# A convolution and a feed-forward block in one kernel: signal parts kept in the signal's place, a joint weight factor, joined butterflies, and the roots of four more row tiles on ScalarE

## The chip, the core and the metric

The kernel runs on one core of one Trainium2 chip. The metric is the device time of one execution in microseconds. Of three runs of the kernel before, the median was 1249.17 us, the lowest 1248.23 and the highest 1249.23. Below, PE is TensorE, DVE is VectorE, ACT is ScalarE, POOL is GpSimd (which here issues the DMAs that add to memory) and SP is the queue that issues all other DMAs.

## The reference

With x = A_q (2048 rows, 1024 columns, float32) and xn its layer norm along the columns, the result is the sum of three terms:

```
y   = causal conv over 2048 rows, per channel, of (short conv of k) * v with ssm_k
out = x + xn * (y + (short conv of k) * v * ssm_D)
        + silu(xn @ w1) @ w2            # w1 1024 x 3584, w2 3584 x 1024
```

The short convolution has four taps per channel. The long one is defined by FFTs of length 4096 along the rows.

## The kernel before, in words

All matmuls take float16 operands; to keep float32 accuracy each operand is stored as two float16 parts, hi and lo (the helper split, L370: ScalarE writes hi, VectorE writes lo = source times scale minus hi), and each product is three matmuls: hi hi, hi lo, lo hi. All instructions are recorded by a small planner written in the kernel (class Order). Each piece of work is a Python generator, a stream, that yields operations with a cost guess; the planner emits, again and again, the stream head that can start earliest, less a bias per stream. Flags and ring buffers with tokens hold a stream back. The order on each engine is thus a result of the planner's costs and of which buffers are free, and it is fixed when the program is built. Since helpers record the instructions, most rows of the profile bear the helper's line: L349 is a tensor_tensor, L352 a scalar_tensor_tensor, L360 an activation, L336 a DMA on SP, L342 a DMA with transpose on SP, L346 a DMA on GpSimd.

**Opening.** ln_rows takes the 16 row tiles of x in groups of 2, 2, 4 and 8. For each tile it forms mean and variance (tiles 4 and 5 on ScalarE, the others on VectorE), then the reciprocal root of the group: for tiles 0 to 3 a Sqrt on ScalarE and a reciprocal on VectorE (L564), for the others an eleven-instruction chain on VectorE (L549 to L559). Tiles 4 to 7 are normalized by ScalarE, the others by VectorE. turned transposes tiles on TensorE into three PSUM buffers ft (L598) and splits them into the operands x2, x3, x4 and so on. Meanwhile the first 8 products of the feed-forward run (plain_unit, L958 to L960), whose results are taken out of the PSUM banks ff by silu. Sqrt and Silu lie in different function tables of ScalarE, so a table load stands between them.

**First matrix product.** units runs it as Strassen-Winograd products P1 to P7 of blocks of x and w1, 12 matmuls of 512 columns each. factors_w1 forms the weight factors (B11; T2 and T3; B21 and B22; T1; T4) for each of 14 pairs of column blocks, stores them in the six buffers wo and keeps a copy in memory for the second half. evacuate copies and combines the products.

**Convolution.** It runs beside the two matrix products, for eight groups g of 128 channels. Per group: loads brings k (kin) and the kernel ssm_k (kf); load_v brings v; gate applies the taps and multiplies by v into acc, and sums squares for the scales; signal_parts splits acc and kf into hi and lo, by DMA transposes via cm; stage1 multiplies them by the transform's matrix on TensorE (L1581 to L1583) and to_spec copies the PSUM tiles into spec and tmp; forward, product and inverse are butterflies and a complex product on VectorE; stage1_inv (L1772 to L1774) transforms back, gated multiplies by the normalized x, and the result is stored or added to out. acc has one buffer; hi and lo have two each, which also serve as the places for quarters of v.

**Second matrix product.** The plain part (L1101 to L1103) and then eight units of P1 to P7 (units2). evacuate2 takes each unit's products out of PSUM: a from P6, d from P5, and direct copies of P2 and P3; they go to half buffers hf (three pairs), and GpSimd adds them to out in memory. In the last unit, direct copies may also use the two pairs ht; d may not (L1214, ws_r is hf).

## Time and profile before

| | |
|---|---|
| median of three runs | 1249.17 us |
| profiled execution, its own time | 1247.09 us |
| its span | 1245.0 us |
| TensorE busy | 1232.0 us, 99% |
| VectorE busy | 1118.5 us, 90% |
| ScalarE busy | 788.4 us, 63% |
| granted TensorE clock, mean | 1.0 |

A row of a timeline gives the start and length in us, the engine, the line, the operation, out and in, how many were merged, and in brackets how long the engine sat idle before it and which instruction or DMA ended that. A row of waits gives who waited for whom, the total, how often, and the longest. A row of groups gives the count, the busy time in us and the mean of one in ns.

### The profile page before, as it was taken

What the parts mean: (1) busy time and instruction counts of PE and PEld (TensorE: products, weight loads), DVE (VectorE), ACT (ScalarE), POOL (GpSimd) and SP (SyncE); (2) the same over time, 40 slices, a digit from 0 to 9 for tenths busy, and PEclk for the clock granted to TensorE, in tenths of its full rate; (3) what the DMA queues carried; (4) which work ended last, traced back from release to release, by engine and by line L of the source; (5) the groups of instructions that cost most, each with busy time, mean ns of one, the idle gap of its engine ahead of it and who ended that gap; (6) DMA issues with size and microseconds to landing.
All of it is one profiled execution on the core that took longest, in us unless ns stands there. A gap on an engine that the chain in (4) does not pass through costs nothing. (4 is left out here: it accounts for less than half of the span.)

```text
span 1245.0 us, 17285 instructions
## 1 busy us (share of the span) xinstructions
PE 1232.0 (99%) x6092; PEld 601.9 (48%) x6092; DVE 1118.5 (90%) x1360; ACT 788.4 (63%) x1431; POOL 83.6 (7%) x93
## 2 busy tenths in 40 slices
PE   9999999999999999999999999999999999999997
PEld 8544444444444544444444544544544444454453
DVE  7999996996999789999999799899999889997981
ACT  7778888876688878669563823753453464554252
POOL 0000000000000000000000000000120030123223
PEclk9999999999999999999999999999999999999999
DMA  9376998879799899859984665579496498978757
GB/s 368 102 263 233 321 302 296 287 233 200 227 327 286 247 294 338 225 168 281 354 304 131 172 214 135 168 263 258 106 225 178 117 195 237 256 142 154 157 121 103
DMA packets 272807, 279.84 MB, mean 225 GB/s; under 512 B 73808, under 2 KB 192848, under 8 KB 271440
## 3 DMA queue, kind: packets, MB, share of 16 engines
q1 hardware_dynamic: 256992, 262.22, 68.2%
q0 software_dynamic: 15728, 16.52, 10.0%
q8 instruction: 47, 0.77, 0.2%
q14 instruction: 40, 0.33, 0.1%
HBM read 175.66 MB, written 88.34 MB: 212 GB/s over the span
## 5 line engine op out<-in xcount | busy, mean ns | idle before, releaser
L1101 PE MATMUL ff<-x,wo 128*128 128x512 f16 x868 | 328.1, 378 | 2.8 <-ACT hf L360 2.2
L1103 PE MATMUL ff<-x,wo 128*128 128x512 f16 x868 | 328.1, 378 | 0.0
L1102 PE MATMUL ff<-x,wo 128*128 128x512 f16 x868 | 328.1, 378 | 0.0
L958 PE MATMUL ff<-x,wo 128*128 128x512 f16 (+1 forms) x808 | 302.8, 375 | 1.3 <-DVE hf L349 0.9
L960 PE MATMUL ff<-x,wo 128*128 128x512 f16 (+1 forms) x808 | 302.8, 375 | 0.0
L959 PE MATMUL ff<-x,wo 128*128 128x512 f16 (+1 forms) x808 | 302.8, 375 | 0.0
L349 DVE TENSOR_TENSOR spec<-spec 128x512 f32<-128x512 f32 (+2 forms) x256 | 261.5, 1052 | 2.1
L1102 PEld LDWEIGHTS <-wo 128*128 128x128 f16 x868 | 84.9, 98 | 101.9 <-issue 3.3
L1103 PEld LDWEIGHTS <-wo 128*128 128x128 f16 x868 | 84.9, 98 | 101.6
L1101 PEld LDWEIGHTS <-wo 128*128 128x128 f16 x868 | 85.8, 99 | 98.8
L960 PEld LDWEIGHTS <-wo 128*128 128x128 f16 x808 | 79.0, 98 | 92.1
L958 PEld LDWEIGHTS <-wo 128*128 128x128 f16 x808 | 80.4, 100 | 87.9
L959 PEld LDWEIGHTS <-wo 128*128 128x128 f16 x808 | 79.0, 98 | 89.8 <-issue 1.9
L349 DVE TENSOR_TENSOR tmp<-spec 128x2048 f32<-128x2048 f32 (+1 forms) x48 | 92.7, 1933 | 0.9
L352 DVE SCALAR_TENSOR_TENSOR ht<-hf,wsc,ht 128x1024 f16<-128x1024 f32 (+1 forms) x56 | 67.3, 1203 | 7.0 <-ACT ht L360 5.3
L360 ACT ACTIVATE ht<-hf,wsc 128x1024 f16<-128x1024 f32 (+1 forms) x56 | 60.8, 1085 | 8.5 <-DMA hs<-ht 3.5
L352 DVE SCALAR_TENSOR_TENSOR wo<-raw,wsc,wo 128x512 f16<-128x512 f32 (+1 forms) x56 | 56.5, 1013 | 7.3 <-ACT wo L360 6.9
L360 ACT ACTIVATE spec<-spec 128x1024 bf16<-128x1024 f32 x32 | 33.7, 1054 | 45.6 <-DVE spec L349 45.6
L352 DVE SCALAR_TENSOR_TENSOR acc<-kin,taps,acc 128x1024 f32<-128x1024 f32 x48 | 61.4, 1279 | 0.6 <-ACT acc L360 0.5
L349 DVE TENSOR_TENSOR spec<-tmp 128x512 f32<-128x512 f32 (+1 forms) x80 | 60.9, 793 | 0.9
L346 POOL DMA_DIRECT2D kf<-in_dskip x8 | 7.4, 922 | 801.8 <-DMA kf<-in_fs 327.2
L346 POOL DMA_DIRECT2D out<-hf x45 | 40.7, 911 | 298.5 <-ACT hf L360 201.8
(193 smaller groups left out, 1798.7 us busy)
## 6 DMA issues: line engine op xcount, KB each, us to landing
wo<-hs SPq DMA_DIRECT2D x160, 256.0 KB, 3.5
hs<-ht SPq DMA_DIRECT2D x80, 256.0 KB, 4.3
raw<-in_w SPq DMA_DIRECT2D x28, 512.0 KB, 5.8
wraw<-in_w SPq DMA_DIRECT2D x24, 512.0 KB, 5.8
w2n<-in_w SPq DMA_DIRECT2D x24, 512.0 KB, 5.9
out<-hf POOLq DMA_DIRECT2D x45, 256.0 KB, 4.3
kin<-in_kp SPq DMA_DIRECT2D x16, 704.0 KB, 5.1
xt<-in_x SPq DMA_DIRECT2D x16, 512.0 KB, 7.4
```

The source lines that it names most:

```text
L346: return Op("POOL", 1.1, 3.0, lambda: nc.gpsimd.dma_start(o, i, accum_op=ADD), [i], [o], m, 2.3 * n)
L349: return V(lambda: nc.vector.tensor_tensor(o, a, b, op=op), o, [a, b], **k)
L352: return V(lambda: nc.vector.scalar_tensor_tensor(o, a, s, b, op0=op0, op1=op1), o, [a, b] + ([] if isinstance(s, float) else [s]), **k)
L360: nc.scalar.activation(o, i, func, scale=scale, **kw)
L958: nc.tensor.matmul(o, w[:, 0, k], xf[:, :, k, 0], start=first and k == 0, stop=False, **kw)
L959: nc.tensor.matmul(o, w[:, 0, k], xf[:, :, k, 1], start=False, stop=False, **kw)
L960: nc.tensor.matmul(o, w[:, 1, k], xf[:, :, k, 0], start=False, stop=last and k == KH - 1, **kw)
L1101: nc.tensor.matmul(po, hx[:, n, 0, :], wc[:, n, 0, :], start=first and n == 0, stop=False, **kw)
L1102: nc.tensor.matmul(po, hx[:, n, 0, :], wc[:, n, 1, :], start=False, stop=False, **kw)
L1103: nc.tensor.matmul(po, hx[:, n, 1, :], wc[:, n, 0, :], start=False, stop=last and n == 3, **kw)
```

## The change

Four things are changed. (1) The roots of row tiles 4 to 7 go to ScalarE and a reciprocal as for tiles 0 to 3, and every Silu waits, in the planner, for that root. (2) T1 is no longer formed in a buffer of its own: B21 and B22 are turned into T4 and T1 by one subtraction of the same T2 from both, and split as one operand of double width; one subtraction per pair goes. (3) One tile sig holds acc and v; the f16 parts of the transposed signal are written over acc, and those of kf over v, by one split of 2048 elements in place of four of 512. v comes in halves, not quarters, and is multiplied and squared in halves. gate and load_v of a group wait for the last matmul of the first stage of the group before. (4) Butterflies on VectorE are joined: the order of the planes in spec (table AT) is changed so that fewer and longer instructions cover the same elements. Besides, in the last unit d may use a half of ht (the function place).

```diff
-ROOTED = 4
+ROOTED = 8
...
-FACTORS = (("B11",), ("T2", "T3"), ("B21", "B22"), ("T1",), ("T4",))
+FACTORS = (("B11",), ("T2", "T3"), ("B21", "B22"), ("T4", "T1"))
...
-    t1_r = Ring(order, rawa, "t1", 1)
...
                 yield V(lambda: nc.vector.reciprocal(r, v), r, [v], us=0.18)
+                if t0 + n == ROOTED:
+                    flag["rooted"].set()
...
             yield from part(("B11",), b[0, 0])
-            yield t1_r.ready
-            t1, t1k = t1_r.tile([P, KH, P])
-            yield v_tt(t1, b[0, 1], b[0, 0], SUB)
             yield v_tt(b[0, 1], b[1, 1], b[0, 1], SUB)
             yield v_tt(b[0, 0], b[0, 1], b[0, 0], ADD)
             yield from part(("T2", "T3"), hv[0])
             yield from part(("B21", "B22"), hv[1])
-            yield from part(("T1",), t1)
-            t1k.set()
-            yield v_tt(b[1, 0], b[1, 0], b[0, 0], SUB)
+            two = hv[1].rearrange("p k (f w) -> p k f w", f=2)
+            yield v_tt(two, two, again(b[0, 0]), SUB)
             toks[0].set()
-            yield from part(("T4",), b[1, 0])
+            yield from part(("T4", "T1"), hv[1])
             toks[1].set()
...
     def silu(i, o, src, tok, done):
+        yield flag["rooted"]
         yield a_act(o, src, AF.Silu, wsc[:, i, 3:4])
...
+        def place():
+            yield lambda: hfs.ready() or last and hts.ready()
+            return (hts if last and hts.ready() else hfs).tile([P, W])
+
         def copied(src, tok, to):
-            yield lambda: hfs.ready() or last and hts.ready()
-            o, otok = (hts if last and hts.ready() else hfs).tile([P, W])
+            o, otok = yield from place()
             yield a_act(o, src, AF.Copy, invc2[:, 0:1])
             tok.set()
...
-        yield ws_r.ready
-        d, dt = ws_r.tile([P, W])
+        d, dt = yield from place()
         yield made["P5"]
         yield a_act(d, two, AF.Copy, invc2[:, 0:1])
...
+    AT = (0, 2, 3, 1, 4, 6, 5, 7)
...
-        kin_r, kf_r, acc_r, hi_r, lo_r = (ring(*a) for a in (
-            ("kin", 1), ("kf", 1), ("acc", 1), ("hi", 2), ("lo", 2)))
+        sig = ra.tile([P, 2, 2, T2, P], F32, name="sig")
+        acc = sig[:, 0]
+        acc16 = acc.bitcast(F16)
+        kparts = sig[:, 1].bitcast(F16).rearrange("p b t w -> p b (t w)").rearrange("p b (q t w) -> p b q t w", q=2, t=T2)
+
+        def signal(t2, q):
+
+            return pair(acc16[:, :, t2, q * P:(q + 1) * P], kparts[:, :, q, t2, :])
+
+        kin_r, kf_r = ring("kin", 1), ring("kf", 1)
...
             for g in range(NG):
-                yield flag["acc", g]
+                if g > 0:
+                    yield flag["stage1", g - 1]
                 for b in range(2):
-                    for q in range(2):
-                        yield lambda: hi_r.ready() or lo_r.ready()
-                        vals[g, b, q] = v, _ = (hi_r if hi_r.ready() else lo_r).tile([P, TQ, P])
-                        yield L(v, vs[g, b][:, q * TQ:(q + 1) * TQ])
-                        flag["v", g, b, q].set()
+                    yield L(sig[:, 1, b], vs[g, b])
+                    flag["v", g, b].set()
...
-                yield acc_r.ready
-                accs[g] = acc, _ = acc_r.tile([P, 2, T2, P])
+                if g > 0:
+                    yield flag["stage1", g - 1]
                 for a in range(2):
-                    yield hi_r.ready
-                    j, tok = hi_r.tile([P, T2, P], BF16)
-                    yield a_act(j, kf[:, a], AF.Square, total=ss[:, 4 + a:5 + a])
-                    tok.set()
-
-                flag["acc", g].set()
+                    j = acc[:, a].bitcast(BF16)[:, 0:TQ].rearrange("p t w -> p (t w)")
+                    yield a_act(j, kf[:, a].rearrange("p t w -> p (t w)"), AF.Square, total=ss[:, 2 + a:3 + a])
...
-                    for q in range(2):
-                        yield flag["v", g, b, q]
-                        v, tok = vals.pop((g, b, q))
-                        o = acc[:, b, q * TQ:(q + 1) * TQ]
-                        yield v_tt(o, o, v, MUL)
-                        yield a_act(v, o, AF.Square, total=ss[:, 2 * b + q:2 * b + q + 1])
-                        tok.set()
+                    yield flag["v", g, b]
+                    v = sig[:, 1, b]
+                    yield v_tt(o, o, v, MUL)
+                    yield a_act(v, o, AF.Square, total=ss[:, b:b + 1])
...
+                whole = [kparts[:, :, q].rearrange("p b t w -> p b (t w)") for q in range(2)]
+                add(split(*whole, kf.rearrange("p b t w -> p b (t w)"), sc[:, 1:2], (ktok, flag["kparts", g])), CB)
                 for t in TO:
+                    there = acc16.rearrange("p b (i t) w -> p (b i) t w", i=2)[:, :, t]
+                    two = [there[:, :, q * P:(q + 1) * P] for q in range(2)]
...
+                        add(split(*two, px.rearrange("p b i w -> p (b i) w"), sc[:, 0:1], (ptok, flag["part", g, t])), CB)
...
                     yield from split(cm[:, 0], cm[:, 1], acc[:, :, t::4, :], sc[:, 0:1])
-                    (hi, htok), (lo, ltok) = part[g, t] = yield from parts_tile(hi_r, lo_r)
-                    flag["part", g, t].n = 3
-                    add(split(hi[:, 1], lo[:, 1], kf[:, :, t::4, :], sc[:, 1:2], (ktok, flag["part", g, t])), CB)
-                    for q, o in enumerate((hi, lo)):
-                        yield X(o[:, 0].rearrange("p b i w -> p (b i) w"), cm[:, q].rearrange("p b i w -> p (b i w)"))
+                    flag["part", g, t].n = 2
+                    for q, o in enumerate(two):
+                        yield X(o, cm[:, q].rearrange("p b i w -> p (b i w)"))
                         ctok.set()
                         flag["part", g, t].set()
...
-                                h, l = hi[:, :, :, i], lo[:, :, :, i]
+                                h, l = (signal(t + 4 * i, q) for q in range(2))
                                 nc.tensor.matmul(o, cf[:, 0], h, start=i == 0, stop=False, **kw)
...
-                    htok.set()
-                    ltok.set()
+                flag["stage1", g].set()
...
-            for o, s, t, r in ((4, 8, 5, -RT), (5, 8, 5, RT), (6, 9, 7, -RT), (7, 9, 7, RT)):
-                flat = [C(a)[:, :, 0].rearrange("p s c w -> p s (c w)") for a in (o, s, t)]
-                yield v_stt(flat[0], flat[1], r, flat[2], MUL, ADD)
+            yield v_stt(long(sp[:, :, 4:6]), long(tmp), -RT, long(sp[:, :, 6:8]), MUL, ADD)
+            yield v_stt(long(sp[:, :, 6:8]), long(tmp), RT, long(sp[:, :, 6:8]), MUL, ADD)
...
-            yield v_tt(C(8, 4, 2), C(0, 4, 2), C(1, 4, 2), ADD)
-            yield v_tt(C(9, 2, 4), pair(C(0)[:, 0], C(5)[:, 0]), pair(C(1)[:, 0], C(4)[:, 0]), SUB)
-            yield v_tt(C(11)[:, 0], pair(I(3), R(2)), pair(I(2), R(3)), SUB)
-            yield v_tt(C(15)[:, 0], pair(I(6), R(7)), pair(I(7), R(6)), SUB)
...
+            yield v_tt(four(8, 11, 12, 14), four(0, 3, 4, 6), four(1, 2, 5, 7), ADD)
+            yield v_tt(C(9, 13), C(0, 5), C(1, 4), SUB)
+            yield v_tt(C(10, 15), pair(turned(3, 2), turned(6, 7)), pair(turned(2, 3), turned(7, 6)), SUB)
+            yield v_tt(C(0, 1), C(8, 9), C(11, 10), ADD)
```

The program has 6016 matmuls before and after, 1211 rows of the recorded order on VectorE become 1100, and 800 plain DMAs on SP become 762. Three places of the order follow, the first and the last on two engines each.

**The opening on ScalarE.** The rows from the last squares of row tile 5 on, before; hf0 is the first Silu's output, nt and ag hold the row statistics, wo3 a weight factor:

```order
L360 ACTIVATE wo2_185<-x1_242,wsc_154 128x512
L360 ACTIVATE ag_429<-nt_430 128x1
L360 ACT_TABLE_LOAD
L360 ACTIVATE hf0_189<-ff1_220,wsc_154 128x512
L360 ACTIVATE wo3_186<-x1_242,wsc_154 128x512
L360 ACTIVATE hf0_189<-ff2_221,wsc_154 128x512
L360 ACTIVATE ht0_192<-hf0_189,wsc_154 128x8x128
L360 ACTIVATE wo3_186<-x1_242,wsc_154 128x512
L360 ACTIVATE xt4_251<-xt4_251,nmr_145,rstd_149 128x1024
L360 ACTIVATE xt5_255<-xt5_255,nmr_145,rstd_149 128x1024
```

and now:

```order
L360 ACTIVATE wo2_174<-x1_231,wsc_143 128x512
L360 ACTIVATE ag_418<-nt_419 128x1
L360 ACTIVATE wo3_175<-x1_231,wsc_143 128x512 x2
L360 ACTIVATE nt_419<-ag_418,eps_153 128x4
L360 ACT_TABLE_LOAD
L360 ACTIVATE hf0_178<-ff1_209,wsc_143 128x512
L360 ACTIVATE xt4_240<-xt4_240,nmr_134,rstd_138 128x1024
L360 ACTIVATE xt5_244<-xt5_244,nmr_134,rstd_138 128x1024
L360 ACTIVATE xt6_248<-xt6_248,nmr_134,rstd_138 128x1024
L360 ACTIVATE xt7_251<-xt7_251,nmr_134,rstd_138 128x1024
```

The root of tiles 4 to 7 (nt from ag) and both splits of wo3 now stand ahead of the table load, and only one Silu is ahead of the applies.

**The same stretch on VectorE, a little later.** The splits of the transposed tiles 6 and 7 into x4 and x5, of which TensorE awaits x4 from ft0, before:

```order
L352 SCALAR_TENSOR_TENSOR x4_482<-ft1_659,x4_482 128x4x128
L352 SCALAR_TENSOR_TENSOR x5_483<-ft2_664,x5_483 128x4x128
L349 TENSOR_TENSOR xt6_259<-xt2_236,xt6_259 128x512
L349 TENSOR_TENSOR xt7_262<-xt7_262 128x512
L352 SCALAR_TENSOR_TENSOR x4_482<-ft0_689,x4_482 128x4x128
L352 SCALAR_TENSOR_TENSOR x5_483<-ft1_697,x5_483 128x4x128
```

and now:

```order
L352 SCALAR_TENSOR_TENSOR x4_471<-ft1_634,x4_471 128x4x128
L352 SCALAR_TENSOR_TENSOR x5_472<-ft2_639,x5_472 128x4x128
L349 TENSOR_TENSOR xt6_248<-xt6_248 128x512
L352 SCALAR_TENSOR_TENSOR ht0_181<-hf0_178,wsc_143,ht0_181 128x8x128
L352 SCALAR_TENSOR_TENSOR x4_471<-ft0_664,x4_471 128x4x128
L352 SCALAR_TENSOR_TENSOR x5_472<-ft1_672,x5_472 128x4x128
```

In place of the sum of tile 7, the lo half of ht0 stands ahead of x4 from ft0.

**ScalarE at the gate of a later group.** The first instructions of the gate of the third group, with the semaphores that each waits for; kf is the convolution's kernel, kin its input, before:

```order
L360 ACTIVATE hi0_4125,css0_4034<-kf_4054 128x1024 [waits DMAHW6_49,DMASW2_49,DVE_49]
L360 ACTIVATE hf2_191<-ff0_3835,wsc_154 128x512 [waits PE_49]
L360 ACTIVATE ht0_192<-hf2_191,wsc_154 128x8x128 [waits DMAHW7_49,Activation_49]
L360 ACTIVATE hi1_4156,css0_4034<-kf_4054 128x1024 [waits DMAHW7_49,DVE_49]
L360 ACTIVATE acc_4124<-kin_3377,taps_173 128x1024
L360 ACTIVATE wraw0_3223,ss2_150<-wraw0_3223 128x1024 [waits DMAHW3_49]
L360 ACTIVATE hf1_190<-hf1_190,wsc_154 128x1024 [waits DVE_49]
L360 ACTIVATE ht1_193<-hf1_190,wsc_154 128x8x128 [waits DMAHW5_49,Activation_49]
```

and now, where sig is acc and v, and spec takes the PSUM tiles of the first stage of the group before:

```order
L360 ACTIVATE hf2_180<-ff3_3690,wsc_143 128x512 [waits PE_49]
L360 ACTIVATE sig_1929,css0_3858<-kf_3261 128x1024 [waits DMASW2_49]
L360 ACTIVATE sig_1929,css0_3858<-kf_3261 128x1024
L360 ACTIVATE sig_1929<-kin_3100,taps_162 128x1024 [waits PE_49,Activation_49]
L360 ACTIVATE hf0_178<-ff0_3754 128x512 [waits PE_49]
L360 ACTIVATE spec_1928<-ps0_3910 128x2x256
L360 ACTIVATE spec_1928<-ps1_3926 128x2x256
L360 ACTIVATE w2n0_1930,ss2_139<-w2n0_1930 128x1024 [waits DMAHW2_49]
L360 ACTIVATE ff3_4001<-ff2_3983 128x512 [waits PE_49]
```

The copy of kin into sig now waits for TensorE, and the copies of ps0 and ps1 into spec follow two rows behind.

**The end, on ScalarE and GpSimd.** ScalarE's copies of the last unit's products; the first row is the copy of P1, and d is the second hf2 before and the first ht0 now. Before:

```order
L360 ACTIVATE ff1_10415<-ff0_10360 128x512
L360 ACTIVATE hf0_189<-ff3_10205,invc2_153 128x512
L360 ACTIVATE hf2_191<-ff1_10415,invc2_153 128x512 x2
L360 ACTIVATE ht0_192<-ff0_10360,invc2_153 128x512
L360 ACTIVATE ht1_193<-ff1_10415,invc2_153 128x512
```

and now:

```order
L360 ACTIVATE ff3_10066<-ff1_10050 128x512
L360 ACTIVATE hf0_178<-ff2_9912,invc2_142 128x512
L360 ACTIVATE hf2_180<-ff3_10066,invc2_142 128x512
L360 ACTIVATE ht0_181<-ff3_10066,invc2_142 128x512
L360 ACTIVATE ht1_182<-ff1_10050,invc2_142 128x512
L360 ACTIVATE ht0_181<-ff3_10066,invc2_142 128x512
```

GpSimd's last outputs, ht with 256x1x128 being the convolution's, before:

```order
L346 DMA out_0<-ht0_192 256x1x128 x2
L346 DMA out_0<-ht1_193 256x1x128
L346 DMA out_0<-hf1_190 128x512
L346 DMA out_0<-ht1_193 256x1x128
L346 DMA out_0<-ht0_192 256x1x128 x2
L346 DMA out_0<-ht1_193 256x1x128 x2
L346 DMA out_0<-hf0_189 128x512
L346 DMA out_0<-hf2_191 128x512 x2
L346 DMA out_0<-ht0_192 128x512
L346 DMA out_0<-ht1_193 128x512
```

and now:

```order
L346 DMA out_0<-ht0_181 256x1x128 x2
L346 DMA out_0<-ht1_182 256x1x128 x2
L346 DMA out_0<-hf2_180 128x512
L346 DMA out_0<-ht1_182 256x1x128 x2
L346 DMA out_0<-hf2_180 128x512
L346 DMA out_0<-hf1_179 128x512
L346 DMA out_0<-hf0_178 128x512
L346 DMA out_0<-hf2_180 128x512
L346 DMA out_0<-ht0_181 128x512
L346 DMA out_0<-ht1_182 128x512
L346 DMA out_0<-ht0_181 128x512
```

Five rows of outputs stood behind the convolution's last, and seven stand there now.

More of the change, by code (lines that the diff above doesn't have):

```diff
@@ L760, in w_part, with again @@
         flag[("w",) + key].set()
+    def again(a):
+        return bass.AP(tensor=a.tensor, offset=a.offset, ap=[list(d) for d in a.ap[:2]] + [[0, 2], list(a.ap[2])])
     def factors_w1():
@@ L1426, in convolution @@
         ctxs["nm"] = py_r
-        kins, kfs, accs, scs, sss, part, ipart, xgs, tmps, vals = ({} for _ in range(10))
+        kins, kfs, scs, sss, ipart, xgs, tmps = ({} for _ in range(7))
         more = {}
@@ L1451, in loads @@
                         yield kf_r.ready
[L1452 removed]
+                        kfs[g] = kf, _ = kf_r.tile([P, 2, T2, P])
                         yield L(kf, fs[g])
@@ L1583, in mm @@
                                 nc.tensor.matmul(o, cf[:, 1], h, start=False, stop=True, **kw)
-                            yield T(mm, ps, [hi, lo], 0.65, m=3.0 if g > 0 and t == TO[0] else 1.0)
+                            yield T(mm, ps, [signal(t + 4 * i, q) for q in range(2)], 0.65, m=3.0 if g > 0 and t == TO[0] else 1.0)
                             (made if i else two[c][3]).set()
-                    htok.set()
-                    ltok.set()
+                flag["stage1", g].set()
         def spare():
@@ L1739, in result_parts @@
                     (hi, htok), (lo, ltok) = ipart[g, t] = yield from parts_tile(more["zh"], more["zl"], (P, 2, 2 * 2 * P))
-                    yield from split(hi, lo, sp[:, 1, t::4].rearrange("p i c w -> p i (c w)"), sc[:, 4:5],
+                    two = pair(sp[:, 1, AT[t]], sp[:, 1, AT[4 + t]]).rearrange("p i c w -> p i (c w)")
+                    yield from split(hi, lo, two, sc[:, 4:5],
                                      (flag["taken", g, t], flag["ipart", g, t]))
```

79 lines of the change are left out of this document (35 added, 44 removed).

## The prediction

> **What bounds the kernel.** I read the page's busy times first, then who TensorE waits for, then the end of the chain that ended last.
>
> ```profile
> span 1245.0 us, 17285 instructions
> PE 1232.0 (99%) x6092; PEld 601.9 (48%) x6092; DVE 1118.5 (90%) x1360; ACT 788.4 (63%) x1431; POOL 83.6 (7%) x93
> ```
>
> TensorE is busy in 99% of the span, but ends of matmuls are modelled, so that alone proves little. Their starts do: in the last unit they stand 0.21 to 0.22 us apart, and the next gap is 2.6 us wide.
>
> ```profile
> 1231.52 0.38 PE L1101 MATMUL ff<-x,wo 128*128 128x512 f16 x1
> 1231.74 0.38 PE L1102 MATMUL ff<-x,wo 128*128 128x512 f16 x1
> 1231.95 0.38 PE L1103 MATMUL ff<-x,wo 128*128 128x512 f16 x1
> 1234.56 0.38 PE L1101 MATMUL ff<-x,wo 128*128 128x512 f16 x1 [2.23 <-ACT hf L360]
> ```
>
> So 1231.95 + 0.216 = 1232.17 was the next start without a wait; 1234.56 - 1232.17 = 2.4 us were lost. The waits of TensorE over the whole span are these:
>
> ```profile
> PE ff L1101 <- ACT hf L360: 2.2, 1, 2.2
> PE ft L598 <- DVE x L352: 1.9, 3, 1.2
> PE ft L1850 <- DVE one L406: 1.2, 1, 1.2
> PE ff L958 <- DVE hf L349: 0.9, 1, 0.9
> PE ps L1581 <- ACT tmp L360: 0.6, 1, 0.6
> PE ff L1101 <- DVE hf L352: 0.6, 1, 0.6
> PE ft L598 <- DVE xt L579: 0.5, 1, 0.5
> PE ff L958 <- ACT x L360: 0.5, 1, 0.5
> PE py L1773 <- DVE zl L352: 0.4, 1, 0.4
> ```
>
> They sum to 8.8 us. The change keeps every matmul, its size and its count (6016 in both programs), so it can gain no more than 8.8 us, 0.7%, plus what lies behind the last matmul, which it leaves. How much work VectorE and ScalarE do matters only where one of them is late for TensorE. I sort the waits into opening (1.9 + 0.5, and 1.2 before the first matmul), middle (0.9 + 0.6 + 0.5 + 0.4 = 2.4) and end (2.2 + 0.6).
>
> **Joined instructions.** Two short ones cost more than one long one:
>
> ```profile
> L349 DVE TENSOR_TENSOR spec<-spec 128x1024 f32<-128x1024 f32 x104 | 125.1, 1219 | 0.6
> L349 DVE TENSOR_TENSOR spec<-spec 128x512 f32<-128x512 f32 x128 | 83.4, 686 | 1.0
> L352 DVE SCALAR_TENSOR_TENSOR zl<-spec,csc,zh 128x1024 f16<-128x1024 f32 x32 | 40.6, 1281 | 8.7 <-ACT zh L360 8.6
> L352 DVE SCALAR_TENSOR_TENSOR lo<-kf,csc,hi 128x512 f16<-128x512 f32 x32 | 23.8, 745 | 0.0
> ```
>
> Counting the instructions of both programs: tensor_tensors of 512 elements fall by 108 and those of 1024 rise by 54, so -108 x 0.686 + 54 x 1.219 = -8.3 us. Splits to f16 of 512 fall by 60, of 1024 rise by 14, and 8 of 2048 come new; the new one is an estimate from the two rows, 1.281 + 2 x 0.536 = 2.35 us, so -60 x 0.745 + 14 x 1.281 + 8 x 2.35 = -8.0 us. The f32 butterflies with a factor go from 32 of 1024 to 16 of 2048, about -2.5 us at the tensor_tensor's slope. With 2 us of root chain (below) VectorE loses 20.7 of 1118.5 us. ScalarE has the other half of each split and half as many squares, so it loses less than VectorE's 20.7, out of 788. None of this is on the path by itself: TensorE covers it at all but the waits above, so I cost it at 0. Without that cover it would be a gain.
>
> **The opening: roots of row tiles 4 to 7.**
>
> ```profile
> 17.77 0.28 ACT L360 ACTIVATE nt<-ag,eps 128x2 f32<-128x2 f32 x1
> 26.64 1.28 ACT L360 ACT_TABLE_LOAD   x1
> 27.93 0.69 ACT L360 ACTIVATE hf<-ff,wsc 128x512 f32<-128x512 f32 x1
> 29.13 0.68 ACT L360 ACTIVATE hf<-ff,wsc 128x512 f32<-128x512 f32 x1
> 31.51 4.62 ACT L360 ACTIVATE xt<-xt,nmr,rstd 128x1024 f32<-128x1024 f32 x4
> 28.72 0.21 DVE L542 BATCH_NORM_AGGREGATE ag<-st 128x2 f32<-128x12 f32 x1
> 31.23 0.16 DVE L572 SCALAR_TENSOR_TENSOR nmr<-ag,rstd 128x4 f32<-128x4 f32 x1
> 32.71 1.28 DVE L352 SCALAR_TENSOR_TENSOR ht<-hf,wsc,ht 128x1024 f16<-128x1024 f32 x1
> 34.51 0.69 DVE L349 TENSOR_TENSOR xt<-xt 128x512 f32<-128x512 f32 x1 [0.52 <-PE ft L598]
> 44.60 1.28 DVE L352 SCALAR_TENSOR_TENSOR x<-ft,x 128x512 f16<-128x512 f32 x2
> 45.43 0.63 PE L598 MATMUL ft<-ident,xt 128*128 128x128 f32 x4 [1.17 <-DVE x L352]
> ```
>
> VectorE's chain lies between the last aggregate (28.93) and nmr (31.23), 2.3 us, and goes but for a reciprocal. ScalarE now waits for that aggregate, roots (0.3, as for two tiles at 17.77), loads the table (1.28), does one Silu (0.6 to the next start): 28.93 + 0.3 + 1.28 + 0.6 = 31.1, so the apply of tile 4 starts 0.4 us earlier than 31.51, not 2. VectorE gains little from it: at 34.51 it waited for TensorE anyway. What is late next is the second Silu and the split of ht0 behind it, which the new order puts in front of the split that TensorE awaits at 45.43: ahead of that split stand the sum of tile 6 and ht0's split (1.19 to the next start) in place of two sums (0.6 each), 0.6 us more, less the 0.3 that VectorE is ahead. I take **+0.3 us**; the bounds are -1.9 (all waits on x go) and +1.2 (the whole ht0 split is added). The second Silu comes later than at 29.13, with its PSUM bank; but 72 full-length matmuls stand before that bank's next use (72 x 0.216 = 15.6 us, so 44.7 at the earliest), and after the applies (36.1) ScalarE has over 8 us for the eight short instructions ahead of the Silu.
>
> **The middle: one place for signal and parts.** The parts go into acc's and v's bytes, so the gate of group g+1 and its v loads wait for the last matmul of the first stage of g. The new order shows ScalarE's first gate instructions ahead of the copies of that same stage's last PSUM tiles, so they wait for the same matmuls. The v loads stand in SP's queue behind that wait too, with the loads of wo after them, which TensorE's progress frees anyway. The transposes by DMA write rows of 256 bytes 2 KB apart instead of adjoining ones; no row has that form, and the nearest is
>
> ```profile
> hi<-cm SPq DMA_TRANSPOSE x28, 3.0
> ```
>
> I take 3.0 us to landing as before; twice that is the upper bound, 3 us later for a quarter of a group, which the order leaves covered unless TensorE stands at that quarter. The four middle waits have no common cause; the first I traced:
>
> ```profile
> 187.33 0.42 SPq L336 DMA_DIRECT2D kf<-in_fs  x1
> 195.77 0.94 POOL L346 DMA_DIRECT2D kf<-in_dskip  x1 [194.46 <-DMA ws_B<-wo]
> 202.24 1.06 ACT L360 ACTIVATE hi<-kf 128x1024 bf16<-128x1024 f32 x1 [2.79 <-DMA kf<-in_dskip]
> 204.01 0.38 PE L958 MATMUL ff<-x,wo 128*128 128x512 f16 x1 [0.46 <-ACT x L360]
> ```
>
> ScalarE stands at kf's square for 2.79 us and TensorE loses 0.46. The same square stays in the new order, one raw weight's square ahead of it, so it may be late again. I take **0 for the middle**, between -2.4 (all go) and +7 (below).
>
> **The end: where the last unit puts d.**
>
> ```profile
> 1216.74 0.69 DVE L349 TENSOR_TENSOR ht<-py,ht 128x512 f32<-128x512 f32 x1 [1.27 <-ACT py L360]
> 1222.60 2.22 POOL L346 DMA_DIRECT2D out<-ht  x2 [2.50 <-issue]
> 1227.61 1.78 POOL L346 DMA_DIRECT2D out<-hf  x2 [2.79 <-issue]
> 1233.83 0.69 ACT L360 ACTIVATE hf<-ff,invc 128x512 f32<-128x512 f32 x1 [8.54 <-DMA out<-hf]
> ```
>
> The chain of waits has between them
>
> ```profile
> 1228.24 5.48 DMA out<-hf
> ```
>
> The last convolution result is done at 1217.4 (1216.74 + 0.69), GpSimd issues its sums to out until 1224.8, so an hf tile's output starts only at 1227.61 and lands at 1233.7. ScalarE's copy of d needs that half of hf; TensorE's P3 needs the copy. After the change d may take a half of ht, and does (the tail in the order). It also comes with less ahead of it: behind the last inverse transform stand 105 full-length matmuls before and 162 after, so the convolution ends 57 x 0.216 = 12.3 us earlier against TensorE, and GpSimd's results with it, near 1224.8 - 12.3 = 1212.5. The last P6 copy (at 1224.60 before) needs an hf half whose output stands first behind them: 1212.5, up to 2.8 for the issue and 5.5 to land make 1220.8, 3.8 us before it is wanted. So the wait of 2.4 us goes: **-2.4 us**, bounds 0 and -2.6. The 0.6 between the halves of P4 stays.
>
> **Sum.** -2.4 + 0.3 + 0 = -2.1 us. Against the profiled execution (1247.09: its span of 1245.0 and 2.1 around it) that is 1245.0. The median of the runs, 1249.17, lies 2.1 above that execution, so I carry the difference over: **1247.1 us**.
>
> [...]
>
> **Rivals.**
> - The rest of the waits goes too. VectorE, the engine behind 0.9 + 0.4 of the middle and all of the opening, has 20.7 us less; middle -2.4 and opening -1.0 with the end -2.4 give 1243.4. For it: the convolution runs up to 12 us ahead. Against it: each of these waits hangs on one late arrival, not on load.
> - VectorE, busy in 90% of the span, is the bound. Then its 20.7 us would come out until TensorE's waits are used up: 1249.17 - 8.8 = 1240.4. Against it: the matmuls' spacing. [...]
> - Slower: the single place of signal and parts. If ScalarE reaches the gate of g+1 before TensorE has finished the first stage of g, all PSUM copies queued behind wait. One product (12 x 0.216 = 2.6 us) covers that; beyond 2.6 us TensorE loses the excess. One excess us in each of the 7 later groups is +7, so 1249.17 - 2.1 + 7 = 1254.1. Against it: ScalarE waits of 2.79 us cost TensorE 0.46 before, and the order puts the gate beside copies that wait for the same matmuls.
> - The end does not change: the d wait goes, but GpSimd's queue, still slow, makes the P6 copy late instead. With the opening's +0.3 it gives 1249.5.
>
> **Chances.** Forecast 0.45, its own range 1245.8 to 1248.5; all waits go 0.24; VectorE's bound 0.03; end unchanged 0.13; slower 0.15. A measurement here can tell about 0.2%, 2.5 us, from no change: below 1246.7 is faster, above 1251.7 slower. A third of the forecast's share, 0.15, lies below 1246.7, so faster 0.15 + 0.24 + 0.03 = 0.42, same 0.30 + 0.13 = 0.43, slower 0.15. The range leaves out VectorE's bound, the far side of all waits going and most of the slower case: 1243.2 to 1251.8.
>
> **What would show it.** No wait of TensorE on ACT hf L360 in the last unit, and the last convolution output on GpSimd near 1212: the end is right. A wait on DVE x near 45 of 1.2 to 1.6 us: the opening. ScalarE waits for TensorE of over 2.6 us ahead of sig<-kin, with TensorE's waits on ff after them: the slower rival. If the convolution's transposes land after 6 us, the middle is wrong. A TensorE wait over 2 us at a new place makes the whole forecast wrong.

## The result, and the profile after

The changed kernel takes 1258.76 us (median of 6 runs, 1257.04 to 1259.92), the kernel before 1249.22 us beside it (6 runs, 1248.23 to 1251.70). The ratio is 1.0072 with a 95% interval of 1.0062 to 1.0083: slower by 9 us (9.5 by the medians), where 1247.1 and a range up to 1251.8 were forecast. The profiled execution took 1258.98 us, with a span of 1257.0. Its span is 12.0 us longer than that of before, more than the medians differ, because the profiled execution of before lies 2.1 us under its median; the account below is of these two executions.

Three lines from the head of the page after:

```profile
span 1257.0 us, 16992 instructions
PE 1237.9 (98%) x6092; PEld 603.1 (48%) x6092; DVE 1104.4 (88%) x1242; ACT 778.7 (62%) x1362; POOL 83.4 (7%) x93
PEclk9999999999999999999999999999999999989999
```

VectorE has 14.1 us less to do (1118.5 - 1104.4), ScalarE 9.7 us less, and the span is 12.0 us longer. The new thing on the page is the 8 in the row of TensorE's granted clock. The longest waits of TensorE after, as "engine, what, line <- what was waited for: us in all, times, longest":

```profile
PE ff L1103 <- ACT x L360: 3.0, 1, 3.0
PE ff L1104 <- DVE x L352: 1.9, 2, 1.6
PE ft L599 <- DVE x L352: 1.7, 1, 1.7
PE ff L1103 <- ACT hf L360: 1.7, 1, 1.7
PE ff L960 <- ACT hf L360: 1.5, 4, 0.7
```

The first two rows did not exist before. They are one place: P4 of the first unit of the second half, whose last quarter waits for the f16 parts of its weight factor (x). In the timeline of TensorE there (start, us, what, wait ahead of it):

```profile
1101.24 0.58 PE L1103 MATMUL ff<-x,wo 128*128 128x512 f16 x1 [3.04 <-ACT x L360]
1103.42 0.59 PE L1104 MATMUL ff<-x,wo 128*128 128x512 f16 x1 [1.59 <-DVE x L352]
1103.80 0.63 PE L1105 MATMUL ff<-x,wo 128*128 128x512 f16 x1
1104.23 0.63 PE L1103 MATMUL ff<-x,wo 128*128 128x512 f16 x1
```

The first wait is put down to ScalarE, which writes the hi part, but ScalarE had itself stood 3.12 us for a subtraction on VectorE:

```profile
1100.47 0.72 ACT L360 ACTIVATE x<-x,tau 128x512 f16<-128x512 f32 x1 [3.12 <-DVE x L349]
```

So both waits are for VectorE. After the second wait the starts are 0.43 us apart and not 0.216: from 1100.70 to 1107.50 us the granted clock was 0.51. To see where the 12 us went I take every step from one matmul's start to the next, subtract the usual step of its kind, and add up what is over 0.15 us (differences are taken before rounding):

| place | before | after | difference |
|---|---|---|---|
| opening, to 50 us | 3.0 | 4.4 | +1.3 |
| middle, 60 to 1070 us | 3.2 | 5.8 | +2.7 |
| P4's factor, 1080 to 1108 us | 0 | 8.4 | +8.4 |
| end, from 1220 us | 3.0 | 2.5 | -0.5 |
| sum | 9.2 | 21.1 | +11.9 |

The 8.4 us are 0.65 + 0.51 just ahead, the two stalls of 3.20 + 1.96, and 2.06 of steps at half clock. So the main question is why that factor is late on a VectorE that has less to do.

### The profile page after: what moved, and what is told of

It is laid out like the page before. It is cut to its first block, busy times and chain, and to the rows that moved or that the text cites. A ratio compares the mean times of both kernels' runs of the same rounds, so it can differ in the third digit from the quotient of the medians.

```text
span 1257.0 us, 16992 instructions
## 1 busy us (share of the span) xinstructions
PE 1237.9 (98%) x6092; PEld 603.1 (48%) x6092; DVE 1104.4 (88%) x1242; ACT 778.7 (62%) x1362; POOL 83.4 (7%) x93
## 4 chain that ended last, share of the span: by engine, by line
PE 64%; DVE 22%; DMA 5%; issue 5%; ACT 3%; SPq 1%; DVEq 0%; ACTq 0%
PE ff L960 10%; PE ff L961 10%; PE ff L962 10%; PE ff L1104 8%; PE ff L1103 8%; PE ff L1105 8%; DVE spec L349 8%; DVE tmp L349 3%; DVE x L352 2%; DVE sig L352 2%; PE ps L1582 1%; PE ps L1584 1%; PE ps L1583 1%; DVE ht L352 1%; DVE spec L352 1%
## 5 line engine op out<-in xcount | busy, mean ns | idle before, releaser
L960 PE MATMUL ff<-x,wo 128*128 128x512 f16 (+1 forms) x808 | 303.2, 375 | 1.9 <-ACT hf L360 1.5
L349 DVE TENSOR_TENSOR spec<-spec 128x1024 f32<-128x1024 f32 (+2 forms) x232 | 259.6, 1146 | 1.8
L960 PEld LDWEIGHTS <-wo 128*128 128x128 f16 x808 | 80.6, 100 | 87.9 <-issue 0.3
L352 DVE SCALAR_TENSOR_TENSOR sig<-kin,taps,sig 128x1024 f32<-128x1024 f32 x48 | 61.5, 1281 | 14.4 <-ACT sig L360 14.4
L352 DVE SCALAR_TENSOR_TENSOR wo<-raw,wsc,wo 128x1024 f16<-128x1024 f32 (+1 forms) x56 | 63.6, 1145 | 7.9 <-ACT wo L360 7.9
L360 ACT ACTIVATE wo<-raw,wsc 128x1024 f16<-128x1024 f32 (+1 forms) x56 | 57.8, 1035 | 10.1 <-DVE raw L349 7.0
```

Of the source, the lines that this page charges most:

```text
L349: return V(lambda: nc.vector.tensor_tensor(o, a, b, op=op), o, [a, b], **k)
L352: return V(lambda: nc.vector.scalar_tensor_tensor(o, a, s, b, op0=op0, op1=op1), o, [a, b] + ([] if isinstance(s, float) else [s]), **k)
L360: nc.scalar.activation(o, i, func, scale=scale, **kw)
L960: nc.tensor.matmul(o, w[:, 0, k], xf[:, :, k, 0], start=first and k == 0, stop=False, **kw)
```

## Why P4's factor is late: two theories

VectorE's timeline after, from the first inverse butterfly of group 6 (spec<-spec of 2048 elements) to the end of P4's last split (the last x<-x,tau,x):

```profile
1087.63 2.29 DVE L349 TENSOR_TENSOR spec<-spec 128x2048 f32<-128x2048 f32 x1
1089.84 0.74 DVE L352 SCALAR_TENSOR_TENSOR x<-wraw,tau,x 128x512 f16<-128x512 f32 x1
...
1091.11 1.22 DVE L349 TENSOR_TENSOR spec<-spec 128x1024 f32<-128x1024 f32 x1
...
1095.69 1.20 DVE L349 TENSOR_TENSOR spec<-spec 128x1024 f32<-128x1024 f32 x1
1096.81 0.74 DVE L352 SCALAR_TENSOR_TENSOR x<-x,tau,x 128x512 f16<-128x512 f32 x1
1097.48 2.35 DVE L349 TENSOR_TENSOR spec<-spec 128x1024 f32<-128x1024 f32 x2
1099.74 0.69 DVE L349 TENSOR_TENSOR x<-wraw,x 128x512 f32<-128x512 f32 x1
1100.35 2.35 DVE L349 TENSOR_TENSOR spec<-spec 128x1024 f32<-128x1024 f32 x2
1102.62 0.75 DVE L352 SCALAR_TENSOR_TENSOR x<-x,tau,x 128x512 f16<-128x512 f32 x1
```

The same place before, and TensorE's use of that split (its second matmul of the last quarter):

```profile
1091.97 0.74 DVE L352 SCALAR_TENSOR_TENSOR x<-x,tau,x 128x512 f16<-128x512 f32 x1
1092.63 2.28 DVE L349 TENSOR_TENSOR spec<-spec 128x2048 f32<-128x2048 f32 x1
```

```profile
1092.78 0.38 PE L1102 MATMUL ff<-x,wo 128*128 128x512 f16 x1
```

Before, the last split stands ahead of the first inverse butterfly; after, 2.29 + 1.22 + 1.20 + 2.35 + 2.35 = 9.4 us of butterflies stand ahead of it. And before, it ended at 1091.97 + 0.74 = 1092.71 and was used at 1092.78: no wait was to be seen, but there was no slack either. VectorE had next to no idle time to make up a delay. From 1040 to 1100 us, in windows of 20, it was busy (third pair of columns) before and after

```profile
1040.00:1060.00 20.00, 20.00 (x96) 9.21 (x95) 19.45 (x28) 9.90 (x22) 0.00 (x0) 1.00 0.73 206
1060.00:1080.00 20.00, 20.00 (x94) 9.05 (x93) 19.93 (x26) 12.25 (x19) 2.60 (x3) 1.00 0.99 270
1080.00:1100.00 20.00, 20.00 (x95) 9.24 (x94) 19.89 (x26) 8.52 (x17) 3.46 (x4) 1.00 0.82 196
```

```profile
1040.00:1060.00 20.00, 20.00 (x96) 9.23 (x94) 19.90 (x26) 11.13 (x21) 0.00 (x0) 1.00 0.70 207
1060.00:1080.00 20.00, 20.00 (x95) 9.06 (x93) 18.83 (x24) 8.26 (x13) 2.59 (x3) 1.00 1.03 234
1080.00:1100.00 20.00, 17.37 (x81) 7.77 (x80) 19.86 (x25) 11.12 (x23) 2.58 (x3) 1.00 1.00 244
```

That is 59.3 and 58.6 of 60 us. The work saved on VectorE was not left free: the convolution runs ahead. The first tap of group 7 starts at 1015.07 us and before at 1024.83, counted on TensorE 64 feed-forward matmuls earlier. What runs ahead stands in front of the splits.

Theory "order": this exchange of rows on a saturated VectorE is the cause. Rival "place": the transposes by DMA into the signal's place are slow, and ScalarE's split of the next part waits for them with the copies of x behind it. There is something in it: 56 transposes land in 3.7 us in the median, against 3.0 and 2.6 before, and ScalarE waited for them 27.5 us against 19.9.

```profile
sig<-cm SPq DMA_TRANSPOSE x56, 3.7
ACT cm L360 <- DMA sig<-cm: 27.5, 14, 5.4
```

and before (with the row of 3.0 that the prediction shows):

```profile
lo<-cm SPq DMA_TRANSPOSE x28, 2.6
ACT cm L360 <- DMA lo<-cm: 19.9, 7, 4.8
```

One such wait reaches VectorE ahead of P4's factor. ScalarE stood 5.42 us for a transpose until 1063.98, and a split behind it let VectorE idle for 1.1 us, the last wait that its rows show before 1103 us:

```profile
1065.35 0.75 DVE L352 SCALAR_TENSOR_TENSOR x<-wraw,tau,x 128x512 f16<-128x512 f32 x1 [1.10 <-ACT x L360]
```

## The experiments

**1. Hold the butterflies back.** The changed kernel, one line more:

```diff
+            if g == 6:
+                yield flag["w2f", "P4"]
             yield v_tt(four(8, 11, 12, 14), four(0, 3, 4, 6), four(1, 2, 5, 7), ADD)
```

> The changed kernel with the same instructions; only group 6's inverse butterflies may not be placed in the order before the last f16 split of P4's second-half factor. Theory 'order': VectorE is busy all through 1040 to 1104 us, and the 9.4 us of inverse butterflies that stand ahead of that split make it late; TensorE's waits there (3.2 + 2.0 us, 0.65 + 0.5 just ahead of them) and the 1.9 us of half clock behind them go, so 1258.8 - 8 = 1251 (1249.5 to 1253). Theory 'place': the transposes into the signal's place, which land in 6.5 us there, make the factor late; they are unchanged, so 1258 to 1260.

1250.91 us, ratio to the kernel before 1.0007 (0.9996 to 1.0017). The wait is gone; VectorE's rows now stand as before, the split first:

```profile
1098.29 0.75 DVE L352 SCALAR_TENSOR_TENSOR x<-x,tau,x 128x512 f16<-128x512 f32 x1 [0.79 <-ACT x L360]
1098.96 2.29 DVE L349 TENSOR_TENSOR spec<-spec 128x2048 f32<-128x2048 f32 x1
```

Same instructions, same transposes (3.8 us to landing), 8 us less. "Place" as the main cause of the late factor has fallen; of the 8.4 us it can have added some 1.1, VectorE's gap at 1065. The 8 us are not all from there: the late wait of the end and the half clock of the opening are gone too (from 46.00 to 49.40 us the granted clock is 1.00, in the changed kernel 0.52), and the middle lost more. This profile lost 5.2 us there to ScalarE's late copies (1.5 in the changed kernel's). At the longest of these waits ScalarE stood 4.8 us for a transpose ahead of the copy that TensorE needed, so there "place" has a share.

**2. Take the joined butterflies apart again**, the rest as changed:

```diff
-            yield v_stt(long(sp[:, :, 4:6]), long(tmp), -RT, long(sp[:, :, 6:8]), MUL, ADD)
-            yield v_stt(long(sp[:, :, 6:8]), long(tmp), RT, long(sp[:, :, 6:8]), MUL, ADD)
+            for o, s, t, r in ((4, 8, 5, -RT), (5, 8, 5, RT), (6, 9, 7, -RT), (7, 9, 7, RT)):
+                yield v_stt(C(o), C(s), r, C(t), MUL, ADD)
...
-            yield v_tt(C(10, 15), pair(turned(3, 2), turned(6, 7)), pair(turned(2, 3), turned(7, 6)), SUB)
+            yield v_tt(C(10), turned(3, 2), turned(2, 3), SUB)
+            yield v_tt(C(15), turned(6, 7), turned(7, 6), SUB)
```

and likewise for C(4, 8) and C(6, 10); the new order of the planes stays.

> The changed kernel with its joined butterflies taken apart again (per group 2 of 2048 elements into 4 of 1024, 3 of 1024 into 6 of 512); the place, the roots, the factors and d stay as changed. VectorE gets some 0.1 us more for each of 5 x 8 instructions, 4 us of busy time. Theory 'order': in its order no inverse butterfly of group 6 stands ahead of the last split of P4's factor, so the late waits go, 1249.5 to 1253 although VectorE has more to do. Theory 'VectorE's load' (more work, more wait): 1260 to 1263. Theory 'place': 1258 to 1260.

1246.78 us, 0.9975 (0.9965 to 0.9984): more instructions, and 12 us less than the changed kernel. The last split stands ahead of the inverse butterflies again, and 0.9 us are lost near P4's factor in place of 8.4, though the transposes took longest here (4.2 us to landing). It came out below the expected band because the wait at the end had gone as well (1.9 us by the starts), and the middle lost 3.4 us less than in the changed kernel.

**3. Roots on VectorE again**, the rest as changed:

```diff
-ROOTED = 8
+ROOTED = 4
...
-        yield flag["rooted"]
```

> The changed kernel with the roots of row tiles 4 to 7 on VectorE again and no wait of the first activation. The opening should get back its 1.2 us (1.9 us wait and a spell of half clock behind it, against 1.3 and none before). Theory 'order': the late wait near 1103 us stays, since the last split of P4's factor still comes late in VectorE's order: 1256 to 1259. A theory that the roots are the whole cause: 1249 to 1250.

1253.61 us, 1.0030 (1.0018 to 1.0042): less than expected. In the opening 1.8 us are lost by the starts, against 3.0 before and 4.4 in the changed kernel. Near 1100 us TensorE still waits for the splits, in pieces, and the granted clock from 1092.40 to 1102.70 us is 0.52; these are the longest waits from 1060 to 1115 us:

```profile
PE ff L1101 <- DVE x L352: 4.6, 4, 1.8
PE ff L1100 <- ACT x L360: 1.1, 2, 0.8
```

By the starts 10.3 us are lost here, more than in the changed kernel, and yet no inverse butterfly stands ahead of the last split. What stands between the splits are rows of the convolution's complex product (at 1092.96, for one), and the first inverse butterfly comes after them all:

```profile
1092.96 2.29 DVE L349 TENSOR_TENSOR tmp<-spec 128x2048 f32<-128x2048 f32 x1
1098.89 0.74 DVE L352 SCALAR_TENSOR_TENSOR x<-x,tau,x 128x512 f16<-128x512 f32 x1
1100.88 2.29 DVE L349 TENSOR_TENSOR spec<-spec 128x2048 f32<-128x2048 f32 x1
```

So the late splits do not hang on the joined butterflies themselves: other long rows of the convolution in front of them do it too. What the expectation had not in it is the wait at the end, which is gone here as well, and a middle that lost 3 us less.

**4. The joined butterflies alone**, in the kernel before (its functions forward and inverse replaced by those of the change, with the table AT):

> The kernel before with the joined butterflies alone. Theory 'order': the last split of P4's factor keeps its place ahead of group 6's inverse butterflies, so no late wait: 1247.5 to 1250.5. Theory 'long instructions' (a butterfly of 2.3 us in place of two of 1.2 holds up the short splits behind it, wherever it stands): late waits as in the changed kernel, 1254 or more.

1247.87 us, 0.9988 (0.9979 to 0.9996). So long instructions are not slow where the order stays good. The joins that cost 12 us on top of the other parts gain 1.5 by themselves. Part of the gain is at the end: the wait of the last unit is gone, though d still goes to hf.

**5. The roots alone**, in the kernel before:

```diff
-ROOTED = 4
+ROOTED = 8
...
+                if t0 + n == ROOTED:
+                    flag["rooted"].set()
...
     def silu(i, o, src, tok, done):
+        yield flag["rooted"]
```

> The kernel before with the roots of row tiles 4 to 7 on ScalarE and the first activation waiting for them, and nothing else. Theory 'local' (an edit costs what its own instructions and waits cost): the opening alone, +0 to +1.5 us, 1249 to 1251. Theory 'order': the later start of the first activation shifts what the planner takes next for the rest of the program, so that splits of other factors come behind other rows of VectorE; waits at places hundreds of us behind the opening, 3 to 9 us in all, 1252 to 1258.

1256.82 us, 1.0060 (1.0045 to 1.0074). An edit of the first 45 us costs 7.5 us, most of it far behind the opening. Of the waits in its profile (an execution 3.3 us above the median), the first stands at inverse transforms between 580 and 1010 us (0.4 us in the kernel before), the second for late copies, 2.0 us of it near 320 us; the third is the opening's.

```profile
PE py L1776 <- DVE zl L352: 4.6, 4, 1.6
PE ff L961 <- ACT hf L360: 2.9, 2, 2.0
PE ft L600 <- DVE x L352: 1.7, 1, 1.7
```

**6. d's place alone**, in the kernel before:

```diff
-        yield ws_r.ready
-        d, dt = ws_r.tile([P, W])
+        d, dt = yield from place()
```

> The kernel before with only the place of d changed (the last unit's d may take a half of ht). The order of all else is the same. If the wait of 2.4 us in the last unit hangs on d's place: it goes, 1246.8 to 1247.5. If another copy into hf is late instead, or the wait comes and goes with the transfers: 1248.5 to 1250.

1245.64 us, 0.9967 (0.9956 to 0.9978). From 1200 us on TensorE has one wait left:

```profile
PE ff L1101 <- DVE hf L352: 0.6, 1, 0.6
```

The profiled execution itself (1247.27 us) is no faster than that of before (1247.09): the wait is gone, but its middle lost 3 us more by the starts.

**7. The single place alone**: the changed kernel with edits 2 and 3, T4 and T1 split apart and d back in hf.

> The changed kernel with all undone but the single place of the signal and the parts, with v's one load and one product: butterflies apart, T4 and T1 apart, roots on VectorE, d in hf. Theory 'order': no inverse butterfly stands ahead of the last split of P4's factor, so no long wait near 1103 us: 1248 to 1251. Theory 'place' (the transposes with rows of 256 bytes 2 KB apart, or the gate that waits for stage 1): 1255 or more.

1250.34 us, 1.0008 (0.9999 to 1.0016). The transposes land in 3.8 us here too, and at 1082 and 1092 us there are two waits of 0.9 and 0.8 us.

**8. Butterflies apart and roots on VectorE**, the rest as changed (edits 2 and 3 together):

> The changed kernel with its joined butterflies apart and the roots on VectorE again; the place, T4 with T1 and d as changed. The opening gives back the 1.2 us (a wait of 1.3 and no half clock, against 1.9 and a spell of it): 1246.8 - 1.2 = 1245.6 if the order near 1103 us stays as good as with the roots on ScalarE; by its order one split of P4's factor comes a little later, so 1245 to 1248. If the roots were worth their 2 us of VectorE: 1248 or more.

1246.78 us, 0.9983 (0.9973 to 0.9993), as experiment 2. The opening's gain is there (1.9 us lost by the starts; the granted clock of the whole execution is 0.999, in the changed kernel 0.995), but this order has a wait of 2.0 us for a copy into hf at 1083 us instead.

**9. Make the kernel before late in the same way.** The control for theory "order": nothing is added but a wait of P4's last split for the sixth inverse butterfly.

```diff
+                if name == "P4" and a == NQ - 1:
+                    yield flag["butterflies"]
                 add(split(wc[:, a, 0, :], wc[:, a, 1, :], src, tau2[:, i:i + 1], toks), 0.05)
...
             yield v_tt(C(2, 2), C(8, 2), C(10, 2), SUB)
+            if g == 6:
+                flag["butterflies"].set()
```

> The kernel before with one thing put in: the last f16 split of P4's factor may stand in the order only behind the first six inverse butterflies of group 6 (2.29 + 3 x 1.2 + 2 x 0.6 = 7.1 us of VectorE; the same instructions, none more). Theory 'order': in the kernel before that split ends at 1092.71 and TensorE uses it at 1092.78, so nothing covers the 7.1 us: TensorE waits 7 us there in one or two pieces, and with a spell of half clock behind it 9: 1256 to 1258.5. If VectorE's rows can be exchanged there without cost (the work is the same, and what TensorE misses there it gets back later): 1249 to 1251.

1254.16 us, 1.0039 (1.0027 to 1.0051). VectorE's six butterflies and the split, then TensorE's wait for it (put down to the instruction that stands next on VectorE):

```profile
1092.53 6.90 DVE L349 TENSOR_TENSOR spec<-spec 128x2048 f32<-128x2048 f32 x6
1099.35 0.74 DVE L352 SCALAR_TENSOR_TENSOR x<-x,tau,x 128x512 f16<-128x512 f32 x1
```

```profile
1093.73 0.38 PE L491 MATMUL py<-css,one 128*128 128x4 f32 x2 [2.50 <-ACT spec L360]
1100.14 0.59 PE L1102 MATMUL ff<-x,wo 128*128 128x512 f16 x1 [3.85 <-DVE pow L495]
```

The first stall is at a small float32 matmul of sums, which the planner now puts ahead of the late split; it only shortens the second, since the split ends at 1100.09 in any case. The two stalls and the spell of half clock behind them (0.51 from 1099.20 to 1106.00 us) come to 9.4 us by the starts, as "order" has it. The run lost less than that and came out below the expected band, because the 2.4 us at the end were gone (0.6 lost there by the starts, against 3.0). That TensorE came to the last unit later, when the outputs had landed, is my reading and was not measured.

**10 to 12. The two parts that gained by themselves**, joined butterflies and d's place, together on the kernel before, and then beside d's place alone:

> The kernel before with the joined butterflies and d's place, the two parts that were worth something by themselves (0.9988 and 0.9967 of the time before). If they add: 0.9955, 1243.9. If both took away the same wait of the last unit (it was gone in the run with the joined butterflies alone as well): 0.9967, 1245.4. If the order turns against it: above 1247.

> The kernel before with d's place alone, once more, on the same chip as the kernel with d's place and the joined butterflies: which of the two is the better one? If the first runs stand: 0.9967 of the time before (0.9956 to 0.9978), 1.9 us under the other.

> The kernel before with d's place and the joined butterflies, once more, beside d's place alone. If the joined butterflies cost something on top of d: 0.9986 (0.9978 to 0.9995) again. If the first difference was the scatter of the runs, both come out alike, near 0.998: their profiled spans were 1243.7 here and 1245.2 with d alone.

Together 1247.39 us, 0.9986 (0.9978 to 0.9995), and again 1247.77, 0.9987 (0.9976 to 0.9998); d alone again 1245.92, 0.9973 (0.9964 to 0.9982). They do not add. Whether both together are worse than d's place alone is open, since the intervals overlap, and the profiles don't settle it: their spans are 1243.7 and 1245.9 for both parts together, 1245.2 and 1244.1 for d alone.

Side by side, as the change of the ratio in per cent:

| kernel | ratio - 1 |
|---|---|
| before + roots | +0.60 |
| before + single place | +0.08 |
| before + joined butterflies | -0.12 |
| before + d's place | -0.33, -0.27 |
| before + joined butterflies + d's place | -0.14, -0.13 |
| before, P4's last split held back | +0.39 |
| all parts (the changed kernel) | +0.72 |
| all parts, butterflies of group 6 held back | +0.07 |
| all parts but the joined butterflies | -0.25 |
| all parts but the roots | +0.30 |
| all parts but both of these | -0.17 |

And where the profiled executions lost their time, by the starts of the matmuls (us):

| kernel | opening | 50 to 1072 | 1072 to 1112 (P4's factor) | end | span |
|---|---|---|---|---|---|
| before | 3.0 | 3.2 | 0 | 3.0 | 1245.0 |
| the changed kernel | 4.4 | 5.8 | 8.4 | 2.5 | 1257.0 |
| butterflies of group 6 held back (1) | 2.8 | 10.4 | 0 | 0.6 | 1250.0 |
| all but the joined butterflies (2) | 4.6 | 2.5 | 0.9 | 0.6 | 1244.8 |
| all but the roots (3) | 1.8 | 2.8 | 10.3 | 0.6 | 1251.9 |
| joined butterflies alone (4) | 3.3 | 3.1 | 1.3 | 0.6 | 1243.4 |
| single place alone (7) | 2.3 | 2.2 | 2.1 | 3.1 | 1246.7 |
| before, last split held back (9) | 2.1 | 3.7 | 9.4 | 0.6 | 1252.3 |

T4 joined with T1 was not run alone. The other four sum to +0.2 to +0.3, the whole is +0.72: parts of this change have no price of their own. The lowest median is that of the kernel before with d's place, 3.3 to 3.8 us under it and 13 under the changed kernel; the changed kernel without the joined butterflies (-0.25) can't be told from it.

## Point by point

- **What bounds the kernel**: right that TensorE's spacing is the bound and that only late arrivals count. VectorE with 14 us less to do did not shorten the span.
- **Joined instructions, cost 0**: this is the step that failed. "TensorE covers it at all but the waits above" was read from waits alone. A place without a wait was taken for a place with cover; at P4's factor the cover was 0.07 us (1092.71 against 1092.78) on an engine busy for 59.3 of 60 us. In place of the 0, the runs showed 8.4 us there once the other parts stood beside the joined butterflies; without the joins 0.9 were left (experiment 2), and delaying the split alone brought 9.4 into the kernel before (experiment 9). The size of the saving was also off (20.7 us estimated, 14.1 measured), which cost nothing. Added up row by row the durations do fall by 19.5 us (1199.1 to 1179.6). But a row starts before the one ahead of it has ended: those of 512 elements last 0.686 us and stand 0.60 apart. With fewer rows there is less of this overlap, so joining two saves less time than their durations suggest.
- **The middle, 0 with a bound of +7 from the gate**: it came to +11.1 (8.4 + 2.7), beyond the bound and by another mechanism. The gate does not hold TensorE up: the single place alone is at 1.0008, and the one wait for the first stage's matmuls that ScalarE has at the signal's place was 0.6 us, where the rival had over 2.6:

```profile
ACT sig L360 <- PE ps L1584: 0.6, 1, 0.6
```

  The loss at P4's factor is a new wait of over 2 us at a new place, which the prediction named as what would overturn it. The new order has it in its rows (butterflies ahead of the last x<-x,tau,x on VectorE), at a place that the prediction did not look at. The other +2.7 is spread over small waits, and no run shows them one cause. The transposes landed in 3.7 us, 0.7 above the value taken, and some copies behind them were late (1.5 us of waits on ACT hf at L960).
- **Opening, +0.3**: it came to +1.3, just over the upper bound of +1.2. The wait for x was 1.7 where 1.2 to 1.6 was expected; the larger part is the half clock after it, which the trace of before, with a wait of 1.2 us, did not show (1.00 from 46.00 to 49.40 us).

```profile
46.00:49.40 3.40, 3.40 (x12) 1.81 (x11) 3.37 (x6) 1.41 (x3) 0.00 (x0) 0.52 0.43 130
```

  In this window of the changed kernel the granted clock (third number from the end) is 0.52.
- **The end, -2.4**: it came to -0.5. Right for d's place by itself (experiment 6: the wait is gone, and the median fell by 3.8; why by more than the 2.4 is open). The convolution did run ahead, though less than forecast: its last sums left GpSimd at 1228.3 (row below), 1216 without the 12 us lost upstream, against 1224.8 before and 1212.5 forecast. In the changed kernel the last unit's wait went, but the unit before, whose copies may only take hf, had one of 1.7 us (1.9 by the starts). GpSimd's row, and then the chain behind that wait, are

```profile
1225.55 2.73 POOL L346 DMA_DIRECT2D out<-ht  x2
```

```profile
1219.05 0.32 SPq L336
1219.54 5.07 DMA ht<-out
1224.61 5.06 DMA out<-hf
1230.36 0.69 ACT hf L360
1231.09 0.38 PE ff L1103
```

  In this chain GpSimd's output of an hf half starts when a load of ht has landed, and ScalarE's two copies into hf, of which TensorE awaits the second, only when that output has. This is the rival of the unchanged end, one unit earlier than I put it: the hf halves behind GpSimd's queue. The wait of the last unit also went without d's place (experiments 4, 5 and 9), so it hangs on a few us of timing as much as on d's place.
- **The rivals**: "the rest of the waits goes too" failed: opening and middle grew. "VectorE is the bound" was given 0.03 and is false for the whole span; in the 60 us ahead of P4's factor it is nearly as full as TensorE (59.3 against 60.0 us in the kernel before), and that was enough. The time that went with it, 1240.4, lies on the wrong side.

That P4's factor is late through the order is shown both ways (experiments 1 and 9). Why the order comes out so, by the convolution's earlier start and the planner's taking whatever can start first, is read from the rows and from the code, not tested by itself.

## What to carry to other kernels

Where one engine is the bound and a second is busy for 59 of 60 us, a place without a wait can have no slack: read the end of each operand against its use before costing an edit on the second engine at nothing. Where a planner sets the order, compare the rows of the nearly saturated engine around every such deadline, since streams that run ahead can come to stand in front of it. Try the parts of a change one by one and all but one: here the lowest median is one part of five, and a part that gained alone cost 12 us in company.

## What the runs showed of the hardware

A stall of TensorE can cost more than itself. With the stalls of 3.2 and 2.0 us near 1100 us the changed kernel's clock was granted at about half, and a window of 6.8 us shows 0.51:

```profile
1100.70:1107.50 6.80, 4.67 (x11) 1.53 (x11) 6.76 (x8) 0.49 (x1) 0.65 (x1) 0.51 0.21 48
```

The starts of the matmuls of 512 columns stand 0.43 us apart there, and 0.216 elsewhere. Other windows with waits in them or just ahead show the like: 0.52 over 3.4 us from 46.00 in the changed kernel, 0.55 over the same window in experiment 2, 0.52 over 10.3 us from 1092.40 in experiment 3 (several waits of 0.4 to 1.8 us), and 0.51 over 6.8 us from 1099.20 in experiment 9.

Not every wait is followed by such a spell. Single waits of 1.74 us at 45 us were, in the changed kernel and in experiment 2; in experiment 1 a wait of the same 1.74 us was followed by a clock of 1.00 from 46.00 to 49.40. Nor did a spell follow the wait of 2.23 us in the kernel before (at 1234.56; 1.00 from 1234 to 1244 us) or that of 2.02 us in experiment 8 (at 1083.42; the next starts stand 0.22 us apart). So the length of a single wait does not tell; what decides is not shown.
